# A chunked recurrence with a spectral mixer behind it: the order of 1,518 operations taken from a table instead of from a planner

## The chip, the core and the metric

The kernel runs on one core of one Trainium2 chip. The metric is device time in microseconds for one execution, the median of several runs. The kernel before has 212.14 us as the median of three runs (211.67 to 212.87).

The core has five instruction streams that matter here: TensorE (PE in the profile, with PEld for its weight loads), VectorE (DVE), ScalarE (ACT), GpSimd (POOL) and SyncE (SP). Each works through its own instructions strictly in the order in which the program lists them. An instruction whose input is not there yet holds up all that stand behind it on the same engine, ready or not. SP does no arithmetic; it issues the loads and stores. POOL issues some loads too, between its own arithmetic.

## What is computed

Two stages follow each other. The first is a recurrence over 768 time steps, for 4 batches and 8 heads with a 40 x 40 state each:

```python
y[:, :, t] = np.einsum('bhd,bhde->bhe', rt, state)
Sa = np.einsum('bhde,bhe->bhd', state, at)
state_decay = state * wt[:, :, None, :] - np.einsum('bhd,bhe->bhde', Sa, bt)
state = state_decay + np.einsum('bhd,bhe->bhde', vt, kt)
```

The second takes the result as x of shape (4, 768, 320), turns it by an angle that it computes from it, and mixes all time steps of a batch:

```python
theta = x @ w_theta
zr, zi = x * np.cos(theta), x * np.sin(theta)
u = x + np.einsum('ts,bsd->btd', w_tok_r, zr) + np.einsum('ts,bsd->btd', w_tok_i, zi)
out = u + np.maximum(u @ w_ch, 0.0)
```

## The kernel before, in words

**Tiles.** Time is cut into chunks of 128 steps, six to a batch, so there are 24 tiles of 128 steps, numbered 0 to 23; tiles 0 to 5 are batch 0. For each tile the kernel loads w, k, b, a and v (160 KB each, `loads`, L638 to L641) and, for every second tile, r in two halves (two times 160 KB for two tiles, L650). Names below such as k3 or `tkb3` mean the load, or the operation, of tile 3.

**The work of one tile.** `prep` (L659) takes the logarithm of w on ACT (`ln`, L665), sums it up along time on PE (`cs`, L672 to L678), takes the exponential on ACT (`exp`, tile ex, L682), adds on DVE (`wi`, tile sx, L685) and takes a second exponential on ACT (`ew`, tile we, L689). The raw k, b and a are scaled with these (`kb`, L696; `ah`, L700) and v is cast (L705). For tiles 0 and 1 this is done on DVE and ACT, for all others on POOL. PE transposes the results (`tkb`, `ta`, `tv`, L622) and ACT copies them out of PSUM (`ekb`, `ea`, `ev`, L625). `scores` (L743) makes four score blocks per tile on PE (`spsi`, `sphi`, `slv`, `slu`, L750), each masked by one DVE operation over 1,024 columns (`mpsi`, `mphi`, `mlv`, `mlu`, L755). `recurrence` (L770) goes from one tile's state to the next one's: `x0` (L783, L789), `nx` on ACT (L795), `nu` (L801), `enu` on ACT (L805), the new state `gt` (L822) with `egt` on DVE (L833 or L841) and, from tile 4 on, `wgt` on POOL (L837). `nut`, `enut` and `slu` lead to `mlu`, and `readout` (L871) makes the tile's result on PE (`y`) and on DVE (`ex`, tile x, L901). `theta` (L913) and `sines` (L923) give cosine and sine on ACT, and POOL multiplies (`z`, tiles zr and zi, L946).

**The rows.** When a whole batch is there, `mix_row` (L954) makes six output rows of 128 steps. Each is six pairs of matmuls on PE (L964, one pair for each of the batch's tiles, called a chunk here), an addition on DVE (`uadd`, L974), transposes (`ut`), a product with w_ch on PE (`ch`, L910), the last addition on DVE (`oo`, L983) and a store on SP (`st`, L986). The token weights are loaded by POOL in twelve blocks of 192 KB (L1004) and transposed on PE (L1012); w_theta and w_ch are loaded by POOL too (200 KB each, L992 and L995).

**What sets the order.** Nothing is issued while `prep`, `recurrence` and the others run. They only call `add`, which notes an operation with its engine, an estimated cost and what it reads and writes; an operation's number is its place in these notes. `Plan.order` (L97) then goes through them as a list scheduler: for each engine it keeps the operations whose inputs are planned, gives each a priority out of `TIMES`, `OFF` and one number per operation in `ADJ`, and picks by priority, by when it estimates an operation could start, and by which of the eight PSUM banks would be free. Two more rules act there: `release` holds back POOL's weight loads, and the soft predecessors of `link` (L71) let an operation that opens a PSUM bank start only when the later users of that bank have their inputs planned as well. For rows, `mix_row` also asks that the chunks 0 to 4 are there before chunk 0 starts. The planned starts are sorted, and the operations are issued in that order (L1055 and following). In the first 14 us PE gets matmuls on a tile of ones (L1064, 68 in all) wherever the plan has idle time.

Of the kernel before, what the change touches and what calls it, by code (L numbers as in the profile page):

```python
# [17 lines left out]
LAT = {("PE", "ACT"): 36, ("PE", "DVE"): 38, ("ACT", "PE"): 52, ("DVE", "PE"): 55,  # L18
       ("POOL", "PE"): 53, ("ACT", "DVE"): 33, ("ACT", "POOL"): 78}
OVERLAP = {"ACT": 102, "DVE": 84, "POOL": 50}  # L20
FREE0 = {"PE": 800.0, "ACT": 2100.0, "DVE": 4400.0, "POOL": 3600.0, "SP": 740.0}
BANKS = 8
DOUBLE = 4
INTO64, OUTOF64 = 95.0, 120.0
SP_DEPTH = 3600.0
FROM_POOL = 4
WARM_FROM, WARM_TO, WARM_STEP = 1450.0, 14000.0, 107.0


class Op:  # L30
    __slots__ = ("eng", "kind", "i", "fn", "cost", "tail", "reads", "writes", "prio",
                 "mode", "table", "new", "spare", "pre", "nsucc", "start", "end", "idx",
                 "npre", "succ", "work", "banks", "soft", "loose", "spec", "release")


class Plan:
# [7 lines left out]
    def add(self, eng, kind, i, fn, cost, reads=(), writes=(), spec=None, mode=128,  # L44
            tail=0, table=None, new=None, spare=0, work=0, after=(), loose=False,
            release=None):
        o = Op()
        o.eng, o.kind, o.i, o.fn, o.cost = eng, kind, i, fn, float(cost)
        o.mode, o.tail, o.table, o.new, o.spare, o.work = mode, float(tail), table, new, spare, float(work)
        o.reads, o.writes, o.loose = reads, writes, loose  # L50
        o.spec, o.release = spec, release
# [19 lines left out]
    def link(self):  # L71
        ops = self.ops
        users = {}
        for o in ops:
            o.succ = []
            o.npre = len(o.pre)
            o.start = o.end = None
            o.banks = None
            o.prio = 1000.0 * (TIMES[o.spec[0]][o.spec[1]] + OFF[o.spec[2]] + ADJ.get(o.idx, 0.0))
            for k in set(o.reads) | set(o.writes):  # L80
                if k[0] == "ps":
                    users.setdefault(k, set()).add(o)
        for o in ops:
            o.soft = set()
            if o.new is not None and not o.loose:
                u = users[o.new[0]]
                o.soft = {p for x in u if x is not o for p in x.pre if p not in u}
                o.soft -= set(o.pre)
            o.npre += len(o.soft)
        for o in ops:  # L90
            for p in o.pre:
                p.succ.append(o)
            for p in o.soft:
                p.succ.append(o)
        return users

    def order(self):  # L97
        ops = self.ops
        users = self.link()
        left = {k: len(v) for k, v in users.items()}  # L100
        home = {}
        bank_free = [0.0] * BANKS
        bank_held = [False] * BANKS
        last_use = {}
        free = dict(FREE0)
        ready = {e: [] for e in free}
        mode = 128
        table = "lnexp"
        dma = 0.0
        est0 = {}  # L110

        def lat(p, o):
            if p.eng == o.eng:
                if p.eng == "PE":
                    return p.start + p.cost
                return p.end + 30
            return p.end + LAT.get((p.eng, o.eng), 45)

        def make_ready(o):
            t = 0.0 if o.release is None else 1000.0 * TIMES["rel"][o.release]  # L120
            for p in o.pre:
                t = max(t, lat(p, o))
            est0[o] = t
            ready[o.eng].append(o)

        for o in ops:
            if o.npre == 0:
                make_ready(o)

        def find(o):  # L130
            n = o.new[1]
            if n == 2:
                c = [(max(bank_free[b], bank_free[b + 1]), (b, b + 1))
                     for b in range(0, DOUBLE, 2)
                     if not bank_held[b] and not bank_held[b + 1]]
                return min(c) if c else None
            c = [(bank_free[b], (b,)) for b in range(DOUBLE, BANKS) if not bank_held[b]]
            return min(c) if len(c) > o.spare else None

        out = []  # L140
        n = len(ops)
        while len(out) < n:
            pick = None
            for e, lst in ready.items():
                if not lst:
                    continue
                te = free[e]
                if e == "SP":
                    te = max(te, dma - SP_DEPTH)
                cand = []  # L150
                lo = None
                for o in lst:
                    t = max(te, est0[o])
                    b = None
                    if o.new is not None:
                        f = find(o)
                        if f is None:
                            continue
                        t = max(t, f[0])
                        b = f[1]  # L160
                    if e == "PE" and o.mode != mode:
                        t = max(t, te + (INTO64 if o.mode == 64 else OUTOF64))
                    cand.append((t, o, b))
                    if lo is None or t < lo:
                        lo = t
                if lo is None:
                    continue
                best = None
                for t, o, b in cand:
                    s = o.prio + WAIT * (t - lo)  # L170
                    if e == "ACT" and o.table is not None and o.table != table:
                        s += TSWITCH
                    if e == "PE" and o.mode != mode:
                        s += PSWITCH
                    if best is None or (s, o.idx) < best[0]:
                        best = ((s, o.idx), t, o, b)
                if pick is None or best[1] < pick[1]:
                    pick = best
            if pick is None:
                raise RuntimeError("no bank: " + str({e: [(o.kind, o.i) for o in l] for e, l in ready.items()}))  # L180
            _, t, o, b = pick
            ready[o.eng].remove(o)
            if o.eng == "ACT" and o.table is not None and o.table != table:
                table = o.table
                t += 1283
            o.start = t
            if o.new is not None:
                o.banks = b
                home[o.new[0]] = b
                for x in b:  # L190
                    bank_held[x] = True
            if o.eng == "PE":
                mode = o.mode
                o.end = t + o.cost + o.tail
                free["PE"] = t + o.cost
            elif o.work:
                free[o.eng] = t + o.cost
                if o.eng == "SP":
                    dma = max(dma, t + 1350.0) + o.work
                    o.end = dma + 600.0  # L200
                else:
                    s = max(t + 1800.0, dma - SP_DEPTH)
                    dma = max(dma, s) + o.work
                    o.end = min(dma, s + 2.0 * o.work) + 1000.0
            else:
                o.end = t + o.cost
                free[o.eng] = o.end - OVERLAP[o.eng]
            for k in set(o.reads) | set(o.writes):
                if k[0] == "ps":
                    left[k] -= 1  # L210
                    last_use[k] = max(last_use.get(k, 0.0), o.end + 50)
                    if left[k] == 0:
                        for x in home[k]:
                            bank_held[x] = False
                            bank_free[x] = last_use[k]
            out.append(o)
            for x in o.succ:
                x.npre -= 1
                if x.npre == 0:
                    make_ready(x)  # L220
        self.home = home
        out.sort(key=lambda o: (o.start, o.idx))
        self.length = max(o.end for o in ops)
        return out
# [5 lines left out]

def tail(n):
    return 166 + n / 2.4 - mm(n)


OFF = dict(
    ah=-52.11, ch=49.75, cs=-52.92, ea=13.09, egd=-104.06, egt=-143.6, ekb=68.26, enu=18.9,
# [7 lines left out]
WAIT, TSWITCH, PSWITCH = 1393.81, 654268.0, -24719.0  # L244
TIMES = dict(
    tile=[
        -86.14, -69.58, -37.21, -14.07, -14.8, 2.38, 2.2, 20.46, 24.1, 33.31, 50.51, 55.4,
        82.34, 92.68, 113.54, 132.24, 115.95, 137.46, 159.05, 157.81, 174.6, 187.04, 146.21,
        211.1],
    row=[  # L250
# [851 lines left out]
```

## Time and profile before

| | |
|---|---|
| median of three runs | 212.14 us (211.67 to 212.87) |
| profiled execution, first to last instruction | 209.9 us |
| what lies around the span, against the median | 2.2 us |
| granted TensorE clock, mean over the span | 0.999 |
| busy: PE / DVE / ACT / POOL | 194.7 / 173.7 / 154.4 / 127.4 us |
| loads on SP's queue, stores with them | 27.54 MB, 66.8% of 16 DMA engines' span |
| loads on POOL's queue | 2.77 MB, 8.6% |
| last input of a tile (b23) lands | 160.9 us |

The profiled execution gives no time of its own beside its span; the 2.2 us is the median less the span. Where the text gives a time for one operation, it is its place in the trace, counted from the first instruction. A line of the trace's order of time gives start, length, engine, line, operation, what it writes and reads, and in brackets the idle time of that engine ahead of it with what ended it.

### The profile page before, as it was taken

How to read it: one execution, taken by the hardware profiler on the slowest of the kernel's cores; microseconds unless marked ns; L12 is line 12 of the kernel's file. 1: busy time of each engine (PE TensorE's matmuls, PEld its weight loads, DVE VectorE, ACT ScalarE, POOL GpSimd, SP SyncE). 2: the span in 40 equal slices, each digit the busy share in tenths (PEclk: the TensorE clock that was granted, in tenths of full speed). 3: DMA queues.
4: the chain of work that ended last, by engine and by line, in shares of the span. 5: the costliest groups of instructions: out<-in, count | busy, mean ns of one | idle time of the engine just before them, and what ended most of it. 6: DMA issues, size and time to landing. Idle time of an engine off the chain costs nothing.

```text
span 209.9 us, 8135 instructions
## 1 busy us (share of the span) xinstructions
PE 194.7 (93%) x3375; PEld 156.5 (75%) x3375; DVE 173.7 (83%) x277; ACT 154.4 (74%) x366; POOL 127.4 (61%) x186
## 2 busy tenths in 40 slices
PE   7778998798999999999999999999999999999993
PEld 7556776577877788888678888778887778877771
DVE  7399967799999797998788778989999987657533
ACT  2686878998799869945987958978799978371211
POOL 3206456879979977875198773786568964614000
PEclk9999999999999999999999999999999999999999
DMA  7999999999999968989999898989894020002122
GB/s 121 200 175 209 185 171 165 204 178 167 188 199 186 199 106 173 164 139 213 163 200 190 176 159 142 197 156 215 190 194 98 0 69 3 31 26 105 40 86 94
DMA packets 134181, 30.82 MB, mean 147 GB/s; under 512 B 125824, under 2 KB 134144, under 8 KB 134144
## 3 DMA queue, kind: packets, MB, share of 16 engines
q1 hardware_dynamic: 131712, 27.54, 66.8%
q0 software_dynamic: 2432, 2.77, 8.6%
q8 instruction: 26, 0.43, 0.9%
q14 instruction: 11, 0.09, 0.1%
HBM read 29.13 MB, written 3.93 MB: 158 GB/s over the span
## 4 chain that ended last, share of the span: by engine, by line
PE 61%; DVE 14%; ACT 10%; POOL 5%; DMA 4%; issue 3%; SPq 0%; POOLq 0%; DVEq 0%; ACTq 0%
PE ps_s L964 15%; PE ps_s L622 10%; PE ps_d L750 9%; PE ps_s L910 8%; PE ps_s L865 3%; DMA wrow_i<-in_moe_w_tok_i_dram 3%; DVE psi L755 3%; DVE lamu L755 2%; DVE phi L755 2%; PE ps_s L801 2%; PE ps_s L894 2%; ACT L934 2%; DMA raw_w<-in_w_dram 2%; DVE lamv L755 2%; PE ps_s L892 2%
## 5 line engine op out<-in xcount | busy, mean ns | idle before, releaser
L696 POOL TENSOR_TENSOR kb<-raw_kb,ex 128x320 bf16<-128x320 f32 x44 | 37.6, 867 | 21.9 <-ACT ex L682 9.0
L964 PE MATMUL ps_s<-zr,wtok_r 128*128 128x320 bf16 x144 | 40.7, 299 | 0.0
L964 PE MATMUL ps_s<-zi,wtok_i 128*128 128x320 bf16 x144 | 40.6, 299 | 0.0
L755 DVE TENSOR_TENSOR psi<-ps_d,mask_p 128x1024 bf16<-128x1024 f32 x24 | 29.2, 1218 | 3.7 <-PE ps_d L750 3.7
L755 DVE TENSOR_TENSOR lamu<-ps_d,mask_p 128x1024 bf16<-128x1024 f32 x24 | 29.2, 1217 | 2.2 <-PE ps_d L750 2.2
L755 DVE TENSOR_TENSOR phi<-ps_d,mask_n 128x1024 bf16<-128x1024 f32 x24 | 29.1, 1214 | 1.3 <-PE ps_d L750 1.1
L755 DVE TENSOR_TENSOR lamv<-ps_d,mask_p 128x1024 bf16<-128x1024 f32 x24 | 29.1, 1213 | 0.4 <-PE ps_d L750 0.3
L946 POOL TENSOR_TENSOR zr<-cs,x 128x320 bf16<-128x320 f32 x23 | 17.9, 793 | 14.1 <-ACT cs L934 14.0
L700 POOL TENSOR_TENSOR ah<-raw_a,we 128x320 bf16<-128x320 f32 x22 | 19.1, 866 | 6.8 <-ACT we L689 3.2
L974 DVE TENSOR_TENSOR u<-ps_s,x 128x320 bf16<-128x320 f32 x24 | 11.6, 488 | 10.7 <-PE ps_s L964 10.7
L946 POOL TENSOR_TENSOR zi<-cs,x 128x320 bf16<-128x320 f32 x23 | 17.9, 795 | 1.3 <-ACT cs L934 1.3
L625 ACT COPY kbT<-ps_s 128x512 f32<-128x512 f32 x24 | 14.2, 592 | 5.7 <-PE ps_s L622 5.3
L750 PE MATMUL ps_d<-aT,kbT 64*128 64x128 bf16 x384 | 17.2, 218 | 0.9 <-ACT aT L625 0.4
L964 PEld LDWEIGHTS <-wtok_r 128*128 128x128 bf16 x144 | 14.1, 98 | 4.2
L625 ACT COPY uT<-ps_s 128x192 f32<-128x192 f32 x24 | 7.5, 320 | 12.8 <-PE ps_s L865 12.5
L964 PEld LDWEIGHTS <-wtok_i 128*128 128x128 bf16 x144 | 14.1, 98 | 3.8
L685 DVE TENSOR_TENSOR sx<-ps_s,lw 128x320 f32<-128x320 f32 x24 | 11.5, 483 | 4.9 <-ACT ex L682 4.8
L622 PE MATMUL ps_s<-ident,kb 128*128 128x128 bf16 x192 | 14.7, 219 | 0.9 <-POOL kb L696 0.6
L892 PE MATMUL ps_s<-kb,lamv 128*128 128x40 bf16 x192 | 15.3, 180 | 0.1
L894 PE MATMUL ps_s<-kb,lamu 128*128 128x40 bf16 x192 | 14.9, 179 | 0.4 <-DVE lamu L755 0.4
L983 DVE SCALAR_TENSOR_TENSOR oo<-ps_s,u 128x320 f32<-128x320 f32 x24 | 11.3, 484 | 4.4 <-PE ps_s L910 4.3
L750 PEld LDWEIGHTS <-kbT 64*128 64x128 bf16 x384 | 11.2, 94 | 4.8 <-issue 1.5
(119 smaller groups left out, 581.7 us busy)
## 6 DMA issues: line engine op xcount, KB each, us to landing
raw_a<-in_a_dram SPq DMA_DIRECT2D x24, 160.0 KB, 4.1
raw_kb<-in_b_dram SPq DMA_DIRECT2D x24, 160.0 KB, 3.8
raw_w<-in_w_dram SPq DMA_DIRECT2D x24, 160.0 KB, 4.1
raw_v<-in_v_dram SPq DMA_DIRECT2D x24, 160.0 KB, 4.1
raw_kb<-in_k_dram SPq DMA_DIRECT2D x24, 160.0 KB, 3.7
raw_r<-in_r_dram SPq DMA_DIRECT2D x24, 160.0 KB, 3.9
out_dram<-oo SPq DMA_DIRECT2D x24, 160.0 KB, 1.9
wrow_r<-in_moe_w_tok_r_dram POOLq DMA_DIRECT2D x6, 192.0 KB, 5.0
```

Of the source, the lines that this page charges most:

```text
L622: nc.tensor.transpose(out=dst[:, c:c + 128], in_=pair(src, g), identity=ident)
L625: nc.scalar.copy(out=out.bitcast(FP32), in_=in_)
L696: lambda j=j: (nc.vector if fast else nc.gpsimd).tensor_tensor(out=paired(kb[:, j])[:, :, :, 0:D], in0=natural(raw_kb[s4][:, j]), in1=invW ...
L700: lambda: (nc.vector if fast else nc.gpsimd).tensor_tensor(out=paired(ah)[:, :, :, 0:D], in0=natural(raw_a[i % 6]), in1=Wi, op=ALU.mult),
L750: nc.tensor.matmul(t[:, q, g, :], lhsT=lhs[rows(q), g * 128:(g + 1) * 128], rhs=rhs[rows(q), g * 128:(g + 1) * 128], start=True, stop=True)
L755: add("DVE", kindm, i, lambda: nc.vector.tensor_tensor(out=dst.rearrange("p a b c -> p (a b) c"), in0=ps(p).rearrange("p a (g c) -> p (a g ...
L892: nc.tensor.matmul(o, lhsT=lamv[:, p, g, :], rhs=kb[:, 0, h, 0:D], start=first, stop=False, skip_group_check=True)
L894: nc.tensor.matmul(o, lhsT=lamu[:, p, g, :], rhs=kb[:, 1, h, 0:D], start=False, stop=True, skip_group_check=True)
L910: nc.tensor.matmul(dst, lhsT=lhs[:, kt, :], rhs=rhs[:, kt, :], start=kt == 0, stop=kt == 2)
L946: nc.vector if fast else nc.gpsimd).tensor_tensor(
L964: nc.tensor.matmul(ps(pk)[:, 0:DM], lhsT=wtok[nm][:, s, j * 128:(j + 1) * 128], rhs=zs[c][:, s], start=n == 0 and c == 0, stop=n == NT - 1 ...
L974: add("DVE", "uadd", q, lambda: nc.vector.tensor_tensor(out=u[:, 0:DM], in0=ps(pk)[:, 0:DM], in1=x[:, 0:DM], op=ALU.add), 488, [pk, ("x", ...
```

## The change

The same 1,518 operations run on the same engines with the same shapes. `Plan.order` no longer plans. It reads the whole order out of a table, and the PSUM bank of each operation that opens one out of a second:

```diff
+ORDER = [
+    0, 2, 1, 3, 6, 19, 7, 20, 5, 21, 4, 22, 12, 24, 23, 25, 8, 26, 28, 9, 30, 29, 31, 53, 11,
+...
+HOMES = [
+    4, 5, 6, 0, 2, 7, 4, 5, 6, 2, 5, 4, 0, 7, 6, 5, 2, 5, 4, 6, 7, 0, 4, 2, 7, 6, 0, 4, 7, 2, 5,
+...
+WARM = {20: 25, 28: 17, 40: 6, 35: 1, 89: 4}
...
     def order(self):
-        ops = self.ops
-        users = self.link()
...
+        at = {n: p for p, n in enumerate(ORDER)}
+        out = [self.ops[n] for n in ORDER]
+        homes = iter(HOMES)
+        self.home = {}
+        for o in out:
             if o.new is not None:
...
+                b = next(homes)
+                self.home[o.new[0]] = (b, b + 1) if o.new[1] == 2 else (b,)
         return out
...
-            if n == 0:
-                need += [e for e in zk if e[3] <= (NT - 2 if bi < B - 1 else NT - 2)]
...
-            add("POOL", "wdma", n, go, 580, [], [(key, 0)], at="rel", work=1030, release=n)
+            add("POOL", "wdma", n, go, 580, [], [(key, 0)], at="rel", work=1030)
...
-    idle = WARM_FROM
-    for o in order:
-        if o.eng == "PE" and o.start < WARM_TO:
-            if o.new is not None:
...
+    for o in plan.order():
+        if o.idx in WARM:
+            t = ps(o.new[0])
```

`TIMES`, `OFF`, `ADJ`, `release`, the soft predecessors and the rule that a row's first chunk waits for four others are gone with the planner. What an operation reads and writes is still noted, and the semaphore waits follow from it as before.

Both programs have 592 PE, 352 ACT, 232 DVE, 174 POOL and 168 SP operations. PE goes over between matmuls of 128 rows and of 64 rows 134 times in both; ACT changes its table 13 times in both after the first load. Half of the operations are at most 3 places from where they stood on PE and SP, 2 on ACT and POOL, 1 on DVE; the farthest move is 35 places on PE and SP, 32 on ACT, 25 on POOL, 10 on DVE. The matmuls on ones go from 68 to 53. The queues begin as follows (`kb` stands once for k and once for b; r is loaded in halves):

```
SP   before  a0 b0 w0 v0 k0 r0 w1 r0 a1 k1 w2 v1 b1 b2 k2 a2 r2 w4 r2 v2 b3 b4 w3 r4 k4 a5 a3 k3 w5 v3 r4 a4 b5 w6 b6 v4
SP   after   w0 b0 k0 a0 r0 w1 r0 v0 w2 k1 b1 v1 w3 a1 k2 b2 a2 r2 r2 w4 v2 a3 r4 r4 b3 k3 b4 w5 k4 w6 a4 v3 v4 a5 k5 b5
POOL before  wth wth kb2 kb2 ah2 r2 v2 kb4 kb4 kb3 ah3 kb3 v3 r4 ah4 ah5 kb5 kb6
POOL after   kb2 kb2 ah2 r2 v2 ah3 r4 kb3 kb3 wth wth kb4 kb4 ah4 v3 v4 ah5 kb5
ACT  before  ln0 exp0 v0 ew0 ev0 ekb0 ea0 ln1 r0 exp1 nx0 er0 er1 enu0 ew1 ln2 enut0 v1 exp2 egd0
ACT  after   ln0 exp0 ew0 ekb0 ea0 ln1 r0 v0 er0 exp1 nx0 ev0 er1 enu0 ln2 enut0 v1 ew1 exp2 ev1
DVE  before  wi0 kb0 kb0 ah0 mpsi0 mphi0 wi1 kb1 mlv0 egt0 ah1 mlu0 kb1 wi2 ex0 mlv1 mpsi1 mphi1 mpsi2 wi4 mphi2 egt1 mlu1 mlv2 ex1 wi3 egt2 mlu2 ex2 wi5 mphi3 mpsi3 mlv3 mpsi4 wi6 mphi4 egt3 mlu3 mlv4
DVE  after   wi0 kb0 kb0 ah0 mpsi0 mphi0 kb1 wi1 kb1 mlv0 mlu0 wi2 egt0 ah1 mlv1 wi3 mpsi1 mphi1 ex0 mpsi2 egt1 mphi2 wi4 mlu1 mlv2 egt2 ex1 mlu2 mpsi3 ex2 wi5 mphi3 wi6 mpsi4 mphi4 egt3 mlv4 mlv3 mlu3
PE   before  cs0 tv0 tkb0 ta0 spsi0 sphi0 cs1 x00 tr0 nu0 slv0 nut0 gt0 cs2 slu0 gd0 tv1 ta1 slv1 y0 tkb1 xt0 spsi1 th0
PE   after   cs0 tkb0 ta0 sphi0 spsi0 cs1 tr0 tv0 x00 nu0 slv0 nut0 cs2 slu0 tkb1 gt0 tv1 slv1 y0 gd0 cs3 ta1 spsi1 tkb2
```

Further on, `cs3` stands at PE's place 20 instead of 42 and `tkb3` at 45 instead of 53; `th0`, the theta of tile 0, moves from place 23 to 58. On SP, the six stores of batch 0 stand behind 83 to 114 of the 144 loads, where they stood behind 74 to 95. Near the end, `th21` stands behind `th22` instead of ahead of it, and the chunks of rows 19 and 20 begin some ten places earlier among those of row 18.

## The prediction

> **What bounds the kernel now.** I read the page's busy sums and slices first, then the table of windows, then the waits and the order of time in the first 45 us.
>
> ```profile
> PE 194.7 (93%) x3375; PEld 156.5 (75%) x3375; DVE 173.7 (83%) x277; ACT 154.4 (74%) x366; POOL 127.4 (61%) x186
> ...
> DVE  7399967799999797998788778989999987657533
> ...
> DMA  7999999999999968989999898989894020002122
> ```
>
> PE is the busiest by far. DMA is full from the second slice to the thirtieth, about 5 to 157 us. Both can't bind at once, so the windows decide; the columns are the stretch, then busy time (and instructions) of PE, PEld, DVE, ACT and POOL, clock, DMA share, GB/s.
>
> ```profile
> 5.00:10.00 5.00, 3.49 (x58) 2.90 (x56) 2.19 (x10) 3.00 (x8) 1.44 (x2) 1.00 1.09 201
> 10.00:15.00 5.00, 3.71 (x77) 2.91 (x75) 4.52 (x6) 4.16 (x11) 0.00 (x0) 1.00 1.05 180
> 15.00:20.00 5.00, 4.29 (x84) 3.23 (x81) 5.00 (x8) 3.09 (x9) 2.70 (x3) 1.00 1.04 210
> 20.00:30.00 10.00, 9.34 (x204) 7.92 (x205) 9.32 (x12) 8.34 (x23) 5.14 (x7) 1.00 0.95 171
> 30.00:40.00 10.00, 7.53 (x147) 5.76 (x144) 7.52 (x9) 8.56 (x19) 6.57 (x11) 1.00 1.00 184
> ...
> 60.00:80.00 20.00, 19.15 (x361) 15.75 (x359) 18.08 (x25) 17.50 (x37) 16.53 (x25) 1.00 0.92 165
> ```
>
> Adding the windows' PE columns, PE is idle 15.3 us of 209.9: 9.7 us before 60 us, 2.1 us from 60 to 200 us, 3.5 us after 200 us. From 60 us on the kernel is bound by PE, which keeps its work (592 operations, 134 changes of row mode in both orders). So an order can win in the first 60 us and hardly elsewhere. There DVE is the fullest engine from 10 to 30 us, loads are in flight without a gap, and what stops PE and DVE is one tile that comes late:
>
> ```profile
> 5.55 0.48 ACT lw L665
> ...
> 30.20 0.49 DVE L901 TENSOR_TENSOR x<-ps_s,we 128x320 bf16<-128x320 f32 x1 [0.75 <-PE ps_s L894]
> 32.54 0.49 DVE L685 TENSOR_TENSOR sx<-ps_s,lw 128x320 f32<-128x320 f32 x1 [1.84 <-ACT ex L682]
> ...
> 40.73 1.22 DVE L755 TENSOR_TENSOR lamu<-ps_d,mask_p 128x1024 bf16<-128x1024 f32 x1 [1.16 <-PE ps_d L750]
> ```
>
> The sx at 32.54 is tile 3's, behind tile 4's and tile 5's work; its w was the 23rd load. POOL says the same of the loads: it waits on what has only just landed.
>
> ```profile
> 25.20 0.86 POOL L696 TENSOR_TENSOR kb<-raw_kb,ex 128x320 bf16<-128x320 f32 x1 [1.29 <-DMA raw_kb<-in_k_dram]
> ...
> 31.40 0.72 POOL L725 CAST r<-raw_r 128x640 bf16<-128x640 f32 x1 [0.72 <-DMA raw_r<-in_r_dram]
> 32.37 0.86 POOL L700 TENSOR_TENSOR ah<-raw_a,we 128x320 bf16<-128x320 f32 x1 [0.25 <-DMA raw_a<-in_a_dram]
> ```
>
> **The rate of the loads.** In the trace the first load lands at 3.61 us and k5, the 38th, at 37.79. Between them lie 31 loads of 160 KB in short runs, 6 halves of r at about 0.5 us each (7.66 after 7.16, 9.83 after 9.35) and w_theta (w1 lands 1.69 us after the load before it, so about 0.8): 34.8 units in 34.2 us, 0.98 us a unit. I count landings in the new order with that.
>
> **Part 1, the start: a gain of 1.3 us.** w0 is issued first and lands at 3.61 instead of 5.53. Rows: `ln` 0.47, then PE from 6.08 to 6.51, so `exp` starts at about 4.6. But DVE clears tiles until 5.50 and can't take `wi0` before, where it took it at 6.99. So 1.49 of the 1.92 us come through, the rest is hidden behind the clearing. k0 and a0 land at 5.6 and 6.5, in time for `kb0` at 5.9 and `ah0` at 6.7. From there the rows of before hold, 1.49 us earlier: first score block at 8.42 instead of 9.90. The new order puts `sphi0` ahead of `spsi0` though DVE masks psi first: 0.2 us back (half of the 0.4 us that the sixteen matmuls step through in the trace). `mpsi0` at 9.14 instead of 10.41. v0, now the eighth load, lands at 9.5, is cast on ACT behind `ln1` and `r0` by 10.0, and `x00` needs `mpsi0` at 10.35: hidden by 0.3 us; every 0.1 us beyond that goes on the path.
>
> The matmuls on ones ahead of `cs0` fall from 45 to 25. In the trace they step by 107 ns until 4.74 us and by 56 ns after it, 3.4 us after the first. 25 of them at 107 ns end at 4.1, `cs0` follows at 4.2, then 17 more: PE stays filled past 4.74 and I charge nothing. If the step stayed at 107 ns, `tkb0` and `ta0` (12 transposes) would take 0.6 us longer; below nothing it can't go. [...]
>
> **Part 2, tiles 0 to 2: the lead shrinks to about 1 us.** By the queue of DVE, 1.22 us a mask (1.13 from one to the next) and 0.4 us a short operation: `mlv0` at 12.6 against 13.62, but `mlu0` waits for `nu0`, `enu0`, `nut0`, `enut0`, `slu0` with only `wi1` and `kb1` ahead of it, an idle time of about 0.75 us that before had filled with `egt0` and `ah1`. `mlv1` then ends at 18.0 instead of 19.14, with `ex0` (0.4 us) still to do: 0.7 us ahead.
>
> **Part 3, tile 3 in its turn: to about 3 us ahead.** w3 is the 13th load (14.4 us; before 23.84), `cs3` and `wi3` stand 22 and 10 places earlier, b3 and k3 are the 25th and 26th (25.2 us; before k3 at 28.90). `kb3` ends on POOL at 26.8 and `tkb3` stands right behind `y1` on PE, so psi of tile 3 can be masked at 28.3. Counted on without a wait, DVE ends `ex2` at 29.9. In the trace of before it had done the same operations plus `wi5`, `mphi3` and `mlv3` at 36.42; less 2.7 us for those three that is 33.7, so the lead is 3.8 us. The idle 0.75 and 1.84 are the larger part of it.
>
> **Part 4, the loads cap it at about 3 us.** POOL issues w_theta after `kb3`, at 26 us: two issues of 0.7 us and 0.8 us of the DMA engines, as before, only later. By the count k4 lands at 28.9, a4 at 30.9 (before 32.24), v3 at 31.9 (30.16, so 1.7 later), v4 at 32.8 (36.48), k5 and b5 at 34.8 and 35.8 (k5 37.79). `mlv3` is moved behind `mlv4`, which covers v3's delay; if it were not covered, DVE would lose 0.5 us or so. With a4, `mpsi4` can't start before 33.5, so DVE idles about 1.5 us around 32; after that no load is late, and `mlv4`, `mlv3`, `mlu3` end at 39.7, against 43.09: 3.4 us. The 1.16 ahead of `lamu` goes, since two masks now stand ahead of it. What is late next is POOL (9.8 of 10 us busy from 50 to 60), so I take 2.8 of the 3.4 as what reaches PE.
>
> **Part 5, from 60 us on: nothing, within a few tenths.** PE is full there, so work that comes earlier is simply done earlier. `th0` moved by 35 places and all moved rows are PE work that stays PE work. The other banks cost by themselves nothing: an opening operation waits only for the last reader of its bank, and PE's waits on a DVE or ACT reader are under 1 us in the list of waits. The stores leave more loads ahead of them:
>
> ```profile
> SPq L986 <- DVE oo L983: 60.1, 17, 10.4
> ```
>
> SP stood 60 us behind stores, up to 10.4 us at a time, with loads queued behind. Loads still landed 0.7 to 32 us ahead of their use after tile 5, so I book no gain. At the end `ut23` now stands ahead of `ch21`, which hides the 0.28 us that `ch23` waited: 0.15 us gained, as `ch22` then waits. Against it, row 19's chunk 3 has 4.7 us of PE work since `th22`, and its z took 4.64 us from `th22` in the trace; with `th21` behind `th22` it comes 0.4 us later: 0.4 us lost.
>
> **The sum.** 2.8 + 0.15 - 0.4, about 2.6: a span of 207.3 instead of 209.9. With 2.2 us around it, the median of the runs shown goes from 212.14 to **209.5 us**. Bounds of the parts: the start 0.7 to 1.5, the stretch to 43 us 1.0 (only the start comes through) to 5.0 (all DVE idle named, 0.75 + 1.84 + 1.16 + 1.3), the rest -1.5 to +0.7. That gives 206.4 to 212.6.
>
> **Rivals.**
> - *Given back.* The early lead is real, but POOL or DVE (10.0 of 10 busy from 50 to 60 us) is what meets the rows, and the lead ends there. Only the start's 1.0 us or nothing is left: 211.2 to 212.5, say 211.8. For it: DVE's and POOL's full windows. Against it: PE is still idle 0.85 us from 60 to 80, and DVE's idle before 45 us shows that it can be ahead too.
> - *Rows wait on z: slower.* The planner let a row start only when chunks 0 to 4 were there; the table doesn't. A chunk at the head of PE's queue whose z is late stops everything. Three places are thin: row 1's chunk 4 (10.6 us of PE work after `th5`, where the last z came 10.0 us after `th5` and POOL now has two weight issues and a `wgt` among the z, 1.9 us), row 7's chunk 3 (9.8 against 7.5), row 19's (above). It costs what POOL is late. From 3 us of lateness in all it eats the gain, and from 4 us the kernel is slower than before by over 0.5%: 213.6. For it: POOL was idle 14.0 us on the sines, up to 6.3 at once. Against it: only tenths are missing at two places, and the third has 2 us to spare.
> - *Everything comes through.* PE takes all DVE idle named, 5 us: 207.1.
>
> **Chances.** The forecast 0.52; everything through 0.16; given back 0.18; rows wait 0.14. The first two are faster by over 0.5% (below 211.1; about what a measurement here can tell from no change), with 0.02 of the lead given back: 0.70. Same: the other 0.16 of it and 0.01 of the rows that wait, 0.17. Slower: the rest of those rows, 0.13. The range goes from the lower bound 206.4 to 213.0, past the given-back case and into the near part of the slower one.
>
> **What will show it.** `ln0` at about 3.7 and the first mask near 9.1; sx of tile 3 near 18 with no wait of 1 us on DVE between 20 and 31; PE idle before 60 us down from 9.7 to about 7; from 60 to 200 us still 2 us. The prediction fails if PE's idle comes back after 60 us at the row matmuls (L964's line of before) with a POOL z as releaser, or if k4, a4 land later than 31 us.

## The result and the profile after

| | before | after |
|---|---|---|
| median, 16 executions each | 212.08 us (211.28 to 213.5) | 210.31 us (208.62 to 211.91) |
| ratio of the times | | 0.9903, 95% interval 0.9877 to 0.9929 |
| profiled execution, first to last instruction | 209.9 us | 206.9 us (its own time 208.62) |
| first sum on PE (`cs0`) | 6.08 us | 4.12 us |
| PE idle before 60 us / 60 to 200 us | 9.7 / 2.1 us | 7.9 / 3.5 us |

Faster by 1.8 us, where 2.6 were forecast (209.5). Two of the sixteen times of the changed kernel, 211.88 and 211.91, lie over 1.5% above its fastest and are left out of the ratio. The profiled execution is the fastest of the sixteen; on its own it gained 3 us of span.

First the page of the changed kernel: busy sums, the slices of DMA, and the chain that ended last.

```profile
PE 192.0 (93%) x3360; PEld 155.9 (75%) x3360; DVE 175.5 (85%) x277; ACT 153.8 (74%) x366; POOL 127.1 (61%) x186
...
DMA  7999999989999999999298879999995001002132
GB/s 118 217 154 205 183 194 156 190 161 163 203 182 149 233 147 231 191 214 177 44 210 180 175 161 222 167 162 196 168 219 124 3 35 36 32 5 95 33 117 106
...
PE 60%; DMA 15%; SPq 7%; ACT 6%; DVE 4%; POOL 3%; issue 3%; POOLq 0%; DVEq 0%; ACTq 0%
```

Two things are new. In the chain, DMA has 15%, where the kernel before had 4%, and SP's queue 7%, where it had 0%. And DMA, full as before, has a hole in the twentieth slice (98 to 103 us): 44 GB/s. Both say where to look: loads. The windows say where PE lost time (columns as before: PE, PEld, DVE, ACT, POOL, clock, DMA share, GB/s).

```profile
10.00:15.00 5.00, 3.61 (x67) 2.71 (x66) 3.88 (x6) 4.21 (x13) 0.00 (x0) 1.00 0.93 153
15.00:20.00 5.00, 3.69 (x67) 2.77 (x67) 5.00 (x7) 2.94 (x7) 3.21 (x4) 1.00 1.03 203
30.00:40.00 10.00, 9.27 (x180) 7.04 (x178) 9.11 (x11) 9.24 (x22) 6.10 (x9) 1.00 1.00 177
...
50.00:60.00 10.00, 8.32 (x176) 7.05 (x174) 9.11 (x12) 8.45 (x21) 6.81 (x11) 1.00 1.07 190
60.00:80.00 20.00, 18.43 (x348) 15.08 (x349) 17.35 (x23) 16.13 (x38) 18.39 (x27) 1.00 1.04 185
...
120.00:140.00 20.00, 18.43 (x339) 15.26 (x338) 16.34 (x23) 16.37 (x38) 9.54 (x14) 1.00 0.92 172
```

From 30 to 40 us, the stretch that the change was to mend, PE has 9.27 of 10 us instead of 7.53. But it is idle 1.68 us from 50 to 60, 1.57 from 60 to 80 and 1.57 from 120 to 140, and POOL, which was full from 50 to 60 us before, now has 6.81.

**The lead.** Idle sums don't show when time was won. So I add up the costs that the kernel itself notes for PE's operations, in the order of each kernel, with 0.106 us for each change between matmuls of 128 and of 64 rows, and compare the times at which the same sum was reached. (In all these traces the median step at such a change is 0.11 us longer than the operation's cost, and 0.00 us longer elsewhere.) The time in the first column is that of the kernel before; the others are the us by which each profiled execution is ahead of it there.

| before at | after | x1: w18 later | x11: and weights later | x6: six a less | x3: new, then old | x4: old, then new |
|---|---|---|---|---|---|---|
| 17.2 | 0.57 | 0.58 | 0.18 | 0.63 | 0.71 | -0.25 |
| 24.6 | 0.14 | -0.33 | -0.62 | -0.63 | 0.10 | -0.22 |
| 40.9 | 3.25 | 2.40 | 2.48 | 1.67 | 2.63 | -0.92 |
| 55.6 | 3.51 | 3.15 | 3.03 | 2.59 | 1.01 | -1.87 |
| 69.4 | 1.77 | 1.59 | 1.92 | 3.73 | 0.87 | -4.53 |
| 87.9 | 1.08 | 1.19 | 1.94 | 2.90 | 0.97 | -5.20 |
| 120.1 | 3.04 | 3.16 | 3.90 | 4.86 | 0.79 | -3.60 |
| 132.2 | 1.27 | 3.13 | 3.87 | 4.32 | 0.77 | -3.98 |
| 157.0 | 1.58 | 3.63 | 3.69 | 4.31 | 0.76 | -3.81 |
| 205.0 | 3.06 | 5.10 | 5.16 | 5.76 | 0.76 | -2.81 |

The changed kernel leads by 3.5 us at 56 us, loses 2.4 by 88, wins 2.0 by 120, loses 1.8 at once and wins 1.8 again. The sum of the last four is small; the forecast had them all at nothing. The last row is the whole gain, but for two columns: x3 has 142 changes of row mode and x4 128, where the others have 134, so that the same sum is not the same work there. By their spans x3 ends 0.1 us behind the kernel before (210.0 us against 209.9) and x4 1.7 us (211.6).

**The first give-back, 57 to 62 us.** PE's two stops, and POOL ahead of them, in the order of time of the changed kernel (start, length, engine, line, operation, in brackets the idle time and what ended it):

```profile
57.62 0.62 PE L450 MATMUL ps_s<-ident,r 128*128 128x128 bf16 x8 [1.07 <-POOL r L442]
61.40 0.40 PE L339 MATMUL ps_s<-ident,ah 128*128 128x128 bf16 x4 [1.99 <-POOL ah L417]
```

```profile
52.51 0.59 POOL L717 DMA_DIRECT2D wrow_i<-in_moe_w_tok_i_dram  x1
53.10 0.54 POOL L717 DMA_DIRECT2D wrow_r<-in_moe_w_tok_r_dram  x1
...
56.84 0.72 POOL L442 CAST r<-raw_r 128x640 bf16<-128x640 f32 x1 [1.01 <-DMA raw_r<-in_r_dram]
59.67 0.85 POOL L413 TENSOR_TENSOR kb<-raw_kb,ex 128x320 bf16<-128x320 f32 x1 [2.11 <-DMA raw_kb<-in_b_dram]
60.48 0.85 POOL L417 TENSOR_TENSOR ah<-raw_a,we 128x320 bf16<-128x320 f32 x1
```

These are tile 8's r (`tr8`) and tile 9's a (`ta9`). `ah9` stood behind `kb9`, which waited for b9 (a9 landed at 59.98, hardly later). PE's rows name POOL, and POOL's rows name DMA. b9 was issued at 52.94 and landed at 59.51, 6.6 us later; in the kernel before it was issued at 51.16 and landed at 54.69. Within 0.5 us of it, at 52.51 and 53.10, POOL issued two blocks of token weights (192 KB each), 3 and 6 us earlier than in the kernel before (55.8 and 59.4 there). They landed 4.8 and 5.7 us after their issue, both ahead of b9, though the second was issued behind it. Between b9's issue and its landing the packets of POOL's queue took 42.3% of the 16 engines' time and those of SP's 65.8%; in the kernel before, between the same two points of its b9, SP's took 104.7% and POOL's none. So in this trace POOL's blocks did not wait for all of SP's loads issued ahead of them, and SP's loads had less of the engines meanwhile.

**The second, 125 us.** `kb17` waits for b17, and on PE `y14` stands behind its transposes. The cause lies 25 us earlier, on SP:

```profile
93.33 0.42 SPq L358 DMA_DIRECT2D raw_a<-in_a_dram  x1
101.04 0.37 SPq L358 DMA_DIRECT2D raw_w<-in_w_dram  x1
```

```profile
124.40 0.85 POOL L413 TENSOR_TENSOR kb<-raw_kb,ex 128x320 bf16<-128x320 f32 x1 [2.79 <-DMA raw_kb<-in_b_dram]
```

The load at 101.04 is w18. It writes a buffer that `ln14` on ACT reads (100.54 to 101.01), and the table puts it at SP's place 91, where it had been at 114. SP can't pass it, so for 7.3 us nothing was issued: the hole in DMA. The list of SP's waits of the changed kernel has it beside the stores' waits, which fell from 60.1 us to 41.1 (it names `aT`, the copy that ACT had begun when `ln14` ended):

```profile
SPq L699 <- DVE oo L696: 41.1, 11, 8.2
SPq L358 <- ACT aT L342: 8.1, 2, 7.5
```

All that stands behind w18 is late by some us: b17 landed at 124.24, and POOL was ready for it at 121.6.

### The profile page after: what moved, and what is told of

Its sections match the earlier page's. It is cut to its first block, busy times and chain, and to the rows that moved or that the text cites. A ratio compares the mean times of both kernels' runs of the same rounds, so it can differ in the third digit from the quotient of the medians.

```text
span 206.9 us, 8111 instructions
## 1 busy us (share of the span) xinstructions
PE 192.0 (93%) x3360; PEld 155.9 (75%) x3360; DVE 175.5 (85%) x277; ACT 153.8 (74%) x366; POOL 127.1 (61%) x186
## 4 chain that ended last, share of the span: by engine, by line
PE 60%; DMA 15%; SPq 7%; ACT 6%; DVE 4%; POOL 3%; issue 3%; POOLq 0%; DVEq 0%; ACTq 0%
PE ps_s L680 17%; DMA raw_kb<-in_b_dram 10%; PE ps_s L339 10%; PE ps_s L627 8%; PE ps_d L467 8%; SPq L358 4%; PE ps_s L582 3%; DMA wrow_r<-in_moe_w_tok_r_dram 3%; SPq L367 2%; DMA raw_a<-in_a_dram 2%; POOL kb L413 2%; PE ps_s L725 2%; PE ps_s L506 2%; PE ps_s L611 2%; PE ps_s L539 2%
## 5 line engine op out<-in xcount | busy, mean ns | idle before, releaser
L413 POOL TENSOR_TENSOR kb<-raw_kb,ex 128x320 bf16<-128x320 f32 x44 | 37.6, 867 | 25.1 <-DMA raw_kb<-in_k_dram 18.4
L680 PE MATMUL ps_s<-zr,wtok_r 128*128 128x320 bf16 x144 | 41.3, 300 | 0.0
L680 PE MATMUL ps_s<-zi,wtok_i 128*128 128x320 bf16 x144 | 41.2, 299 | 0.0
L339 PE MATMUL ps_s<-ident,kb 128*128 128x128 bf16 x192 | 15.2, 220 | 1.8 <-POOL kb L413 1.8
L554 POOL TENSOR_TENSOR gt<-sum,ex 128x320 bf16<-128x320 f32 x13 | 9.4, 724 | 11.2 <-DVE sum L550 11.1
L618 DVE TENSOR_TENSOR x<-ps_s,we 128x320 bf16<-128x320 f32 x24 | 11.7, 486 | 4.6 <-PE ps_s L611 4.5
## 6 DMA issues: line engine op xcount, KB each, us to landing
wrow_i<-in_moe_w_tok_i_dram POOLq DMA_DIRECT2D x6, 192.0 KB, 4.7
```

Of the source, the lines that this page charges most:

```text
L339: nc.tensor.transpose(out=dst[:, c:c + 128], in_=pair(src, g), identity=ident)
L413: lambda j=j: (nc.vector if fast else nc.gpsimd).tensor_tensor(out=paired(kb[:, j])[:, :, :, 0:D], in0=natural(raw_kb[s4][:, j]), in1=invW ...
L618: add("DVE", "ex", i, lambda: nc.vector.tensor_tensor(out=x[:, 0:DM].rearrange("p (c g d) -> p g c d", c=2, g=G), in0=ps(pk)[:, 0:DM].rear ...
L680: nc.tensor.matmul(ps(pk)[:, 0:DM], lhsT=wtok[nm][:, s, j * 128:(j + 1) * 128], rhs=zs[c][:, s], start=n == 0 and c == 0, stop=n == NT - 1 ...
```

## Experiments

Twelve kernels, in three series; each series has its own runs of the kernel before (medians 211.96, 212.06 and 212.26 us), and each ratio is against those. In the expectations a "stop" is the step from one PE operation's start to the next, less the first one's own cost; the idle time in the brackets above is about 0.2 us less for the same stop.

### w18 at a later place

The changed kernel's order, with one load moved eight places on SP:

```diff
 SP  ... w14 b14 k14 st0 a14
-w18
 k15 st2 r14 w16 k16 b16 v15 w17
+w18
 r14 b15 a16 st3 ...
```

> The changed kernel with one load moved: w of tile 18 is issued 8 places later on SP's queue, behind w of tile 17. In the changed kernel it stood at the queue's head from 93.8 to 101.0 us waiting for ln of tile 14, and DMA ran dry (44 GB/s in one slice). Theory (loads bind in places): PE's 1.74 us stop ahead of y14 at 125.5 us goes; PE idle from 120 to 140 us falls from 1.57 to under 0.4 us; about 1.5 us faster than the changed kernel, ratio to the kernel before 0.982 to 0.986. Rival (PE has enough other work, SP's wait costs nothing): the stop moves elsewhere, ratio 0.990 as the changed kernel.

Measured: 207.58 us, 0.9762 (0.9724 to 0.9799). SP now issues a14, k15, st2 and r14 from 93.74 to 97.90 with no wait over 2.6 us, w18 goes out at 103.72, b17 lands at 120.14. The window of 120 to 140 us of this kernel:

```profile
120.00:140.00 20.00, 20.00 (x375) 16.57 (x372) 18.09 (x25) 17.44 (x41) 10.05 (x15) 1.00 0.96 179
```

PE is full there, and the lead stays at 3.13 where the changed kernel fell to 1.27. The theory holds. The gain is larger than expected: the lead at the end is 2.0 us higher, and the medians are 2.7 apart (in two series). By the medians, one load moved by 8 places is worth more than the 1.8 us of the whole change.

### The start alone, and the start undone

The kernel before, but with w0 loaded first and 25 matmuls on ones ahead of `cs0` instead of 45:

```diff
-SP  a0 b0 w0 v0 k0 ...       ones ahead of cs0: 45
+SP  w0 a0 b0 v0 k0 ...       ones ahead of cs0: 25
```

> The order of before, with w of tile 0 issued first and 25 instead of 45 matmuls on ones ahead of cs0; nothing else. Prediction's part 1 (a start 1.3 us earlier that is kept): ratio 0.994. Theory after the two traces (the lead of 1.95 us at the first matmul was down to 0.14 us after 12 us of PE work, since the next tiles' loads are no earlier): cs0 near 4.1 us, and nothing left at the end, ratio 0.998 to 1.001.

Measured: 212.37 us, 1.0004 (0.9975 to 1.0034). `cs0` starts 2.0 us earlier, and then PE waits 2.5 us for `tv0`, the next in its order, which starts at 6.86. By 17 us the lead is -0.05. In the changed kernel `tv0` stands six operations further back. A second cost of this start: in this trace the matmuls keep stepping by 107 ns through `tkb0` and `ta0`, and still do at 9.4 us, where in the kernel before the full rate came at 4.8. The other way round, the changed kernel with w0 third:

```diff
-SP  w0 b0 k0 a0 ...          ones ahead of cs0: 25
+SP  b0 k0 w0 a0 ...          ones ahead of cs0: 45
```

> The changed kernel with w0 loaded third again, as in the kernel before (b0 k0 w0 a0), and 45 ones ahead of its first sum as there. Theory (the new order's time is set by loads at 57 to 62 and 125 us, which don't start earlier for w0 being first; the 1.95 us of the start are down to 0.1 by 24 us anyway): 0.988 to 0.993 of before, as the changed kernel. Rival (the prediction's part 1: 1.3 us are kept): 0.995 to 0.999.

Measured: 210.53 us, 0.9895 (0.9849 to 0.9941), the same as the changed kernel's 0.9903. So of the 1.3 us at the start nothing is seen at the end, alone or with the rest; the interval leaves room for up to 0.8 us.

### One half of the order at a time

x3 takes the first 340 operations (to about 50 us) from the new order and the rest from the old, x4 the reverse; banks go with their half (in words; the kernels hold the finished tables):

```diff
 x3:  ORDER = new[:340] + [n for n in old if n not in new[:340]]
 x4:  ORDER = old[:340] + [n for n in new if n not in old[:340]]
```

> The first 340 of 1,518 operations in the new order (up to about 50 us), the rest in the old one. Theory (the new order wins about 3 us by 50 us, and what of it is lost later is lost to the loads): the lead over before at equal PE work is 2.5 to 3.5 us at 48 us and 1 to 2 us behind 63 us; ratio 0.990 to 0.995. Rival (the gain at the end is made by the later order alone): ratio 0.998 to 1.002.

> The first 340 operations in the old order, the rest in the new one: the complement of the kernel with the new order first. Theory: no lead at 50 us; the later order gains about 1.4 us from 80 us on and loses 1.7 us at tile 17's load again, ratio 0.994 to 1.001. Rival (the gain at the end is made by the later order alone): ratio 0.990.

Measured: x3 212.74 us, 1.0011 (0.9984 to 1.0038); x4 212.29 us, 0.9984 (0.9946 to 1.0022). The expectation of x3 missed, and the figure of its rival is right: the early part by itself gives nothing. Its lead is 2.63 at 41 us and 1.0 from 56 us on, and in time that 1.0 is next to nothing: 0.85 of it are the 8 changes of row mode that x3 has more, at 0.106 us each. The first 340 operations hold 46 of them in the new order and 39 in the old, the rest 87 and 95; x3 takes the larger number of both. The remainder goes at once, 1.66 us ahead of the transposes of `kb8` at 53.68. But b8 and k8 had landed by 51.1; POOL had other work of the old order ahead of `kb8`. So x3 shows that the old rest can't use the lead; it doesn't show loads as the reason, and the seam itself, where the two halves meet, may be it. In x4 the new rest, reached without the lead, runs into late loads, k9 and r8, issued at 55.36 and 56.41 and so again next to the two weight blocks (55.52 and 56.11); k9 needed 6.8 us from issue to landing:

```profile
62.33 0.85 POOL L413 TENSOR_TENSOR kb<-raw_kb,ex 128x320 bf16<-128x320 f32 x1 [3.43 <-DMA raw_kb<-in_k_dram]
```

PE stops 2.8 us ahead of `tr8`, whose cast stood behind that `kb`, and right after it the clock was halved for 3.4 us (last section). x4 is 5.2 us behind at 88 us; by the table's sum it regains 2.4 by the end, by the spans, which its fewer changes of row mode help, 3.5. So the later part of the new order is by itself faster by 2 us or more, and not by nothing. Neither half wins alone.

### Are loads the cap?

Both orders without six loads of a:

```diff
     add("SP", "l" + key[0][4:], i,
+        (lambda: None) if key[0] == "raw_a" and 6 <= i < 12 else
         lambda dst=dst, src=src: nc.sync.dma_start(out=dst, in_=src),
         ...
```

> The changed kernel without the six loads of a for tiles 6 to 11 (160 KB each; those tiles then use the a that lies in the buffer). This takes 6 units of about 0.98 us from the DMA engines between about 33 and 60 us, and nothing from any other engine. Theory (the lead of 3 to 4 us that the new order has at 56 us is given back because the loads are late): kb9 and r8 land 2 us or more earlier, the stops ahead of tr8 and ta9 (1.26 and 2.17 us) go, the lead past 64 us stays at 3 us or more, and the time is 0.975 to 0.984 of before. Rival (POOL, with 9.8 of 10 us busy there, is what sets it): the stops stay within 0.5 us of what they were, 0.987 to 0.993.

> The kernel before, without the same six loads of a for tiles 6 to 11. It says how much of the gain of x6_new_without_six_a belongs to the fewer loads alone, whatever the order. Theory (in the kernel before these loads are not late where PE needs them; the bound there is what DVE had lost before 45 us): 0.995 to 1.001 of before. Rival (loads bind the kernel before in the same way): 0.984 to 0.992, and the new order then has no larger need of the loads than the old one.

Measured: x6 207.03 us, 0.9771 (0.9737 to 0.9805); x7 212.28 us, 1.0016 (0.9996 to 1.0035). The same relief is worth 1.3% in the new order (0.9903 to 0.9771) and nothing in the old. In x6, the window and POOL at the place of the first give-back:

```profile
50.00:60.00 10.00, 10.00 (x213) 8.39 (x213) 10.00 (x13) 9.37 (x25) 9.73 (x16) 1.00 0.98 179
```

```profile
56.60 0.71 POOL L443 CAST r<-raw_r 128x640 bf16<-128x640 f32 x1
57.28 0.86 POOL L414 TENSOR_TENSOR kb<-raw_kb,ex 128x320 bf16<-128x320 f32 x1
58.11 0.86 POOL L418 TENSOR_TENSOR ah<-raw_a,we 128x320 bf16<-128x320 f32 x1
```

No bracket stands behind them: nothing is waited for. PE, DVE and POOL are all full. POOL at 9.73 of 10 us lets PE have 10.00, so POOL was not the cap, against the rival of this run and against the prediction's rival "Given back". The new order has turned a kernel that waited for its own order into one that waits for its loads around 60 us. Whether the DMA engines or SP's queue make them late x6 can't tell, as it relieves both; x11 below moves loads of POOL alone.

### The weights and b9: four versions of one place

All four on top of x1. Two edits: b9 ahead on SP, and POOL's two weight loads further back.

```diff
 SP    ... k7 v6 a7 w9 b8 k8
+b9
 a8 v8 v7 k9 r8 r8
-b9
 a9 v9 b10 ...
 POOL  kb8 kb8 ah8
-wtok wtok
 v8 v7 wch kb9
+wtok wtok      (x9, x11)
 r8 kb9
+wtok wtok      (x5)
 ah9 ...
```

x5 has b9 ahead and the weights behind the second kb9; x9 b9 ahead and the weights between the two; x10 only b9; x11 only the weights, between the two kb9.

> The order of x1_w18_later (0.976 of before), with b9's load moved ahead on SP to right behind k8's, and POOL's two loads of the second block of token weights moved from ahead of r8's cast to behind kb9. Theory (what is left of the give-back at 57 to 62 us is b9 and r8 landing late, pushed back by the 384 KB of weights and by b9's later place): the stop ahead of ta9 (1.3 us in x1) goes, the one ahead of tr8 (1.9 us) shrinks to under 1 us, the lead at 64 us of PE work is 2 us or more above x1's 1 to 2, and 1 to 2 us of it reach the end: 0.967 to 0.973 of before. Rival (the DMA engines are full there, so that b9 and r8 earlier make a8, v8 or k10 late): the stops only change their names, 0.974 to 0.978. Second rival (the weights come too late for the transposes of the second block): a new stop at those transposes, 0.978 to 0.985.

> As x5_b9_and_weights, but POOL issues the two loads of token weights (192 KB each) between the two kb9, ahead of r8's cast, about 55.8 us, where x5 issued them at 58.45 and 59.04 and PE then stood 3.8 us ahead of their transposes at 62.53. Theory (x5 lost only by that one stop; its b9 and r8 were in time): the weights land at 59 to 60 us, the stop ahead of the transposes is under 1 us, those ahead of tr8 and ta9 stay at about 1.2 and 0.3 us, the lead at 64 us of PE work is 2 us or more above x1_w18_later's, and the time is 0.966 to 0.974 of before. Rival (the DMA engines are full, so whatever is put ahead makes something else late by as much): 0.974 to 0.980, no better than x1's 0.976.

> x1_w18_later with b9's load moved ahead to right behind k8's, POOL as in x1. Theory (loads are in a line; one ahead puts a8, v8, v7, k9 and r8 back by 0.98 us each): the stop ahead of ta9 goes (1.3 us in x1), the one ahead of tr8 grows from 1.9 to about 2.9, so nothing is gained: 0.973 to 0.979 of before. Rival (only b9 was late, r8 has room): 0.966 to 0.972.

> x1_w18_later with the two loads of token weights issued between the two kb9, SP as in x1. Theory: r8's second half lands about 0.8 us earlier, b9 still late; the stop ahead of tr8 falls from 1.9 to about 1.1, that ahead of ta9 stays near 1.3: 0.970 to 0.976. Rival (the weights now are late at their transposes): 0.976 to 0.984.

Measured:

| | us | against before |
|---|---|---|
| x1 | 207.58 | 0.9762 (0.9724 to 0.9799) |
| x5 | 211.28 | 0.9964 (0.9942 to 0.9986) |
| x9 | 210.6 | no interval; six times from 207.36 to 212.51 |
| x10 | 207.62 | 0.9759 (0.9713 to 0.9804) |
| x11 | 206.28 | 0.9711 (0.9671 to 0.9751) |

x10 went as its theory said in time, though not in detail: `kb9` was no longer late, r8's stop shrank to 0.4 instead of growing, and now a9 was late (60.24, behind the same weights): 1.66 us. Here the load put ahead moved the wait to the next one. x11 takes what lies between away, the weights, and POOL finds r8, b9 and a9 landed:

```profile
56.05 0.60 POOL L717 DMA_DIRECT2D wrow_i<-in_moe_w_tok_i_dram  x1
56.64 0.54 POOL L717 DMA_DIRECT2D wrow_r<-in_moe_w_tok_r_dram  x1
57.17 0.74 POOL L442 CAST r<-raw_r 128x640 bf16<-128x640 f32 x1
57.86 0.87 POOL L413 TENSOR_TENSOR kb<-raw_kb,ex 128x320 bf16<-128x320 f32 x1
58.68 0.87 POOL L417 TENSOR_TENSOR ah<-raw_a,we 128x320 bf16<-128x320 f32 x1
```

b9, issued at 53.70, landed in 3.8 us; the expectation had it late still. The price is a stop of 1.4 us ahead of the weights' transposes, and 1.1 us ahead of `tr8` remain. It is the fastest version of all; its interval overlaps x1's, and in its own series it is 1.3 us below x10.

x5 and x9 missed. In x5 the weights came 3.8 us too late for PE, the second rival of its expectation, but at a price that it had not: 211.28 us is 3.7 above x1, where it expected 0.4 to 2. In x9, `kb9` waited until 56.98, since k9 had been put back by the loads ahead, and the weights stood behind it on POOL, and r8's cast, landed since 57.68, behind the weights. Both then show this (x9, the same columns; the eighth from the left is the clock that the throttle granted):

```profile
58.00:60.00 2.00, 0.29 (x6) 0.30 (x7) 1.04 (x1) 1.97 (x3) 2.00 (x4) 1.00 0.94 144
60.00:62.00 2.00, 1.12 (x18) 0.85 (x15) 0.49 (x1) 0.37 (x1) 1.92 (x3) 0.60 1.09 186
62.00:64.00 2.00, 1.94 (x22) 1.36 (x24) 1.01 (x2) 0.00 (x1) 2.00 (x4) 0.50 1.22 216
64.00:66.00 2.00, 2.00 (x32) 1.75 (x32) 1.25 (x2) 1.31 (x4) 1.25 (x3) 0.50 1.19 191
66.00:68.00 2.00, 2.00 (x46) 1.70 (x42) 1.63 (x3) 1.92 (x4) 0.18 (x1) 0.70 1.00 182
```

After a stop of 2.1 us, PE's clock is halved from 60.4 to 67.2 us, and PE is "full" from 62 to 66 us with 22 and 32 instructions, where x1 has 55 and 40. What that is worth stands in the last section.

### Other banks

In words (the kernel holds a finished table of banks):

```diff
-b = next(homes)                         # the table's bank
+b = the bank that has been free longest # 249 of 448 differ
```

> The changed kernel's order, instruction by instruction, but each operation that opens PSUM banks takes the one that has been free the longest: 249 of the 448 choices differ from the changed kernel's (317 differ between before and after). Theory (the banks of the table cost and gain nothing by themselves; a choice that is the longest free can only wait less): 0.986 to 0.993, as the changed kernel with its 0.990. Rival (the table's banks are a part of the gain): 0.995 to 1.0. Other rival (the table's banks hold the order back): below 0.984.

Measured: 210.11 us, 0.989 (0.9858 to 0.9922), against 0.9903 for the changed kernel. The banks are worth nothing that can be measured, as the prediction had it. (Its profiled execution is its longest, 211.91 us, and isn't compared here.)

## Why the prediction was right, and where not

- **Part 1, the start: right, and worth nothing.** w0 landed at 3.58 (3.61 forecast), the first mask started at 8.77 (9.14). x2 and x12 show nothing of it at the end. "PE stays filled past 4.74" did not bring the faster step: the 17 ones behind `cs0` still step by 107 ns, up to 6.3 us, where before the step fell to 56 at 4.74. But "I charge nothing" held in this order. `tkb0` begins at 6.31 and steps by 56 ns; it takes 0.78 us instead of 0.45 (8.34 to 8.79 before) since its second half waits for DVE's second `kb`, which ends at 6.64. In x6 the ones step by 56 ns from 4.8 us on, and `tkb0` is no earlier or shorter. Below are the ones, DVE's two `kb` and `tkb0` of the changed kernel, then `tkb0` of x6:

```profile
4.54 1.93 PE L774 MATMUL ps_s<-busy 128*128 128x128 bf16 x17
...
5.76 0.88 DVE L413 TENSOR_TENSOR kb<-raw_kb,ex 128x320 bf16<-128x320 f32 x2
...
6.31 0.78 PE L339 MATMUL ps_s<-ident,kb 128*128 128x128 bf16 x8
```

```profile
6.29 0.80 PE L339 MATMUL ps_s<-ident,kb 128*128 128x128 bf16 x8 [0.49 <-DVE kb L414]
```

Nor did the number of ones decide when the full rate came: with 25 ones ahead of `cs0` it came at 6.3 us (changed kernel), 4.8 (x6) and after 9.4 (x2), with 45 at 4.8 (before) and 6.6 (x12). In x2, where PE ran dry behind the ones, the slow step that Part 1 names as its risk did come.
- **Part 2, the lead shrinks: the size nearly right, by luck.** It fell to 0.6 at 17 us and 0.1 at 25 us (0.7 to 1 forecast), for another reason. `mlv0` started at 13.46, not 12.6 (13.62 before): it was not `mlu0` that waited for `nut0` but `kb1` ahead of both, for b1. This was the first sign of what followed:

```profile
13.05 0.49 DVE L413 TENSOR_TENSOR kb<-raw_kb,ex 128x320 bf16<-128x320 f32 x1 [1.12 <-DMA raw_kb<-in_b_dram]
```

- **Part 3, tile 3 in its turn: right, a bit less.** Tile 3's sx starts at 18.55, no wait of DVE between 20 and 31 us exceeds 0.24 us, psi of tile 3 is masked at 29.32 (28.3 forecast), the x of tile 2 ends at 31.27 (29.9). By the prediction's own count against 33.7 that is a lead of 2.4 us on DVE, not 3.8.

```profile
18.55 0.47 DVE L402 TENSOR_TENSOR sx<-ps_s,lw 128x320 f32<-128x320 f32 x1
...
29.32 1.22 DVE L472 TENSOR_TENSOR psi<-ps_d,mask_p 128x1024 bf16<-128x1024 f32 x1
30.78 0.49 DVE L618 TENSOR_TENSOR x<-ps_s,we 128x320 bf16<-128x320 f32 x1 [0.24 <-PE ps_s L611]
...
38.89 1.22 DVE L472 TENSOR_TENSOR lamu<-ps_d,mask_p 128x1024 bf16<-128x1024 f32 x1
```

- **Part 4, 2.8 us at 43 us: the size was right there.** k4, a4, v4, k5 landed at 28.2, 30.7, 32.8, 35.8 (28.9, 30.9, 32.8, 34.8 forecast); `mlu3` ended at 40.11 (39.7). PE had 3.25 us of lead at 41 us and 3.5 at 56. The step that failed is its sentence "after that no load is late". The count of landings stopped at k5. b9, r8 and, by SP's queue, b17 were late. The row of POOL's `kb` has 18.4 of 25.1 us of idle time that ended with a load, but 13.4 of them are the wait of the very first one, to 16.28 us (8.9 us in the kernel before, to 16.00). From 20 us on, 10.0 of 11.1 us ended with a load, where in the kernel before it was 1.3 of 12.7.

```profile
L413 POOL TENSOR_TENSOR kb<-raw_kb,ex 128x320 bf16<-128x320 f32 x44 | 37.6, 867 | 25.1 <-DMA raw_kb<-in_k_dram 18.4
```

- **Part 5, nothing from 60 us on: wrong in its terms, nearly right in its sum.** It has -2.4 (b9 and r8), +2.0 (88 to 120 us), -1.8 (w18) and +1.8 (132 us to the end) where it booked 0.15 - 0.4. The two gains were missed because "PE is full" was read from busy time. In the traces a matmul's busy time reaches over the next one's start (the first one of `cs0` in the changed kernel lasts 0.45 us from 4.12, and the next starts at 4.36), so steps that are 0.1 to 0.4 us too long don't show as idle. The sum of PE's steps less the operations' own costs was 5.3 us from 80 to 125 us before and is 3.5 now without the stop at b17, 4.3 and 2.6 from 158 us on; the changes of row mode in these stretches, 27 and 18 before, 24 and 16 now, are a part of it. The page fits: PE's busy sum fell from 194.7 to 192.0 us with the same 592 operations and 15 ones less. The two losses were missed because I took landings of 0.7 to 32 us ahead of their use in the old order as slack that the new one keeps (r20 and r22 had even there only 0.1 us); the new one uses data 3.5 us earlier, and moves loads of its own. The sign "from 60 to 200 us still 2 us" of PE idle failed with 3.5.
- **The rivals.** "Rows wait on z" did not happen; the row matmuls have no idle time ahead of them in the changed kernel either. "Given back" came in part, by another cause than the one named: not POOL or DVE, as x6 shows, but what POOL waits for. "Everything comes through" needed 5 us; x1 and x11 lead by 5.1 and 5.2 at the end of their traces, so the order holds that much once a load or two stand elsewhere.

```profile
L680 PE MATMUL ps_s<-zr,wtok_r 128*128 128x320 bf16 x144 | 41.3, 300 | 0.0
```

- **The median.** From the median before, 212.1, to its own profiled execution, 208.62, the gain was 3.5 us, by the medians 1.8. A part of the difference is the clock, below; that the profiled execution is the fastest of sixteen is another.

## What to carry to other kernels

When an order frees the engines, the loads that were in time can become the bound, as here: count landings as far as the lead reaches, not as far as the change does, and count loads of both queues. In an in-order load queue, the place of a load is set by when its buffer is free as much as by when its data is wanted; one load that is too early stops all behind it (7.3 us here, 2.0 us at the end of the trace). Compare the steps of the fullest engine, not its busy share: 2 us were hidden in windows that showed 19.4 to 20 of 20. And when two orders are joined, count first what each half brings along, here the changes of row mode, before the time is read as that of a half.

## What the runs showed of the hardware

**After some stops of 2 us or more on PE the clock was halved, and 1.7 or 3.4 us were not granted.** In the profiled executions of x4, x5, x9 and x12, the clock that the throttle granted fell to 0.50 in a stop of 2.1 to 3.8 us or up to 1.7 us after it, for 3.41 us (x4 from 64.4, x12 from 64.6) or 6.83 us (x5 from 61.6, x9 from 60.4). What was not granted is 1.71, 1.71, 3.41 and 3.41 us: in these four one or two times the same amount. No fall followed the stops of 1.7 to 2.2 us in x10, x1 and the changed kernel's profiled execution. Between two changes of the clock lie 13.65, 54.61, 58.03, 139.95 or 143.36 us at the full rate (x4, x5, x6, x9, x12), which are 4, 16, 17, 41 and 42 times 3.413 us (143.36 / 42). Laid on a grid of that step, the 3.413 us right before the fall have PE busy for 0.21 (x5), 0.23 (x4), 0.43 (x9) and 0.51 (x12) of their length; the thinnest such stretches with no fall behind them have 0.52 (x11), 0.53 (x1), 0.53 and 0.54 (the changed kernel). That it depends on how a stop of 2 us lies to such a grid whether the clock falls is an estimate from these shares. A sharp limit near one half isn't shown: in x6 the clock fell after a stretch of 0.67, in x8 not after one of 0.49 but only after the next, of 0.37 (at 63.8 us).

At the start, too, the same matmuls met the full rate at different times: with 45 ones from the same 1.46 us on, it came at 4.8 us in the profiled execution of the kernel before and at 6.6 in that of x12. The column of the granted clock has 1.00 there in both; in these first microseconds the step of the matmuls (107 ns, then 56) tells, not the column.

It also shows in the times. Of the fourteen executions of the changed kernel that the ratio counts, the nine with a mean granted clock of 0.996 or more have a median of 209.72 us, the five with 0.992 or less 210.93; 1.71 us not granted in 209 us are 0.8%. Of 63 executions of the kernel before, three have 0.992 or less; of x5, x9 and x12, all 24. So the new order's late loads seem to cost twice in some executions, once as a stop and once as a slow clock; the traces of x4, x5, x9 and x12 show both. Where the clock was halved in the executions without a trace is open: in x6 it was from 18.4 to 21.9 us, so the thin stretch from 10 to 20 us (PE 7.3 of 10 us in the changed kernel, 7.4 in x6) is a second candidate. That x6 is among the fastest with it fits an early lead that is lost anyway.

**Open.** How much of the early lead the old rest could keep without x3's 8 further changes of row mode was not tried. Nor was it tried whether x11's remaining stops (1.1 and 1.4 us) go with a smaller block of weights.
